# Softmax attention beside a SwiGLU feed-forward on one core: odd score pairs in two single PSUM banks, and a plan of 108 blocks in place of 115

## The chip, the cores and the metric

The kernel runs on one core of one Trainium2 chip. The metric is device time in microseconds (us), the median of several executions. The engines that matter here are TensorE (PE in the profile; PEld is its loading of weights), ScalarE (ACT), VectorE (DVE), GpSimd (POOL) and SyncE (SP), whose queue issues most DMA transfers. PSUM, where matmuls leave their results, has eight banks of 512 float32 values per partition.

## What is computed

The input `x` has 2048 rows (tokens) of 512 features. With `xn` the layer-normed `x`, the output is `x + s * g`:

```python
qkv = xn @ wqkv                           # 32 heads, 16 features each
p = softmax(q @ k.T * 16 ** -0.5)         # per head, 2048 x 2048
s = (p @ v, heads side by side) @ wo
g = silu((silu(xn @ w_gate) * (xn @ w_up)) @ w_down)   # 512 -> 1792 -> 512
```

All tensors are float32. The feed-forward and the projections use matmuls on a high and a low part of each operand (three products for one), so that a reduced-precision pass gives nearly full precision.

## The kernel before

**Stages.** A prologue (the first score matmul is at 157.6 us) normalises `x`, transposes it and projects q, k and v to DRAM. A long middle stretch runs attention and the feed-forward together on TensorE. A short tail does the last quarter of the output projection.

**Attention.** The heads are taken four at a time (8 groups), the queries 512 at a time (4 blocks of queries); one such combination is a *unit*, and there are 32. A unit goes over 16 *key tiles* of 128 keys. For each key tile there are two *pairs* (j = 0, 1; "even" and "odd" below) of two heads each. The two scores of a pair are two matmuls that run at the same time, on the upper and the lower half of the array's rows (line 899), one PSUM bank each. ScalarE turns scores into exponentials in SBUF (`pr`). Then `values` (line 423) multiplies the exponentials of a key tile with v: four heads at once in the four column quarters of the array, in float32, accumulated in the bank `acc`.

**PSUM in the middle stretch.** `bankx` and `banky` belong to the feed-forward, `acc` to `values`. `score[0]` and `score[1]` have two banks each: even pairs go to `score[0]`, odd pairs to `score[1]`. `spare` is one bank. An ordinary pair is read by one ACTIVATE over both banks, 128x1024 (line 902). A pair that is `apart` (the last of its block, or one in `shared`) puts its first half in `room[:, 0]` and its second half in `spare`, and each half is read for itself, 128x512.

**Kept-back halves.** For a pair in `shared`, one half gets no exponential at once: VectorE copies the scores to SBUF (line 907) so that the bank comes free, and ScalarE does that exponential from SBUF at the end of the block (line 920, after the loop over pairs). This is the second half of the pair, or the first half if the pair is the block's last.

**Fills.** The feed-forward is a generator; `fill(n)` draws n *fills* from it, each a pair of 64-row matmuls into `bankx` and `banky` (line 237). An up unit (one slice of 128 of the 1792 hidden features) has 24 fills and ends in a tanh on ScalarE (line 264) and four VectorE operations (lines 265, 266, 230, 231). A down unit (128 tokens through `w_down`) has 21. At the start of an up unit VectorE splits the next gate and up weights (`split_gu`, lines 198 and 199), and after eight fills it splits a slice of `w_down` (`split_wd`, lines 208 and 209). A down unit that finishes its 128 tokens leaves `store_gate` in `after` (a tanh on ScalarE, a multiply on VectorE, a store on GpSimd's queue); the last four leave `next_out` as well, which splits parts for the output projection on VectorE. `catch_up` runs what is in `after` before pair 2 of the next block.

**Blocks and the plan.** The stretch is cut into *blocks* of 2 to 6 key tiles of one unit. In a block, TensorE does: scores of pairs 0 and 1; `values` of the block before; then pairs 2 to the last, and after pair n the number of fills `parts[n]`. So ScalarE works off pairs 0 and 1 and the kept-back halves of the block before while TensorE is in `values`. Below, a *turn* is the passage through `values`: into it after pair 1, and out of it to pair 2. I write (k, n) for a block of k key tiles and n fills. `plan()` chooses the blocks by dynamic programming: 327 per block, plus `short(k, n)` for a block with few fills for its tiles, or a small price where the table `SHARED` has an entry for (k, n), which says which pairs are shared and where the fills go. Without an entry the fills are spread evenly. The planner's rule, followed through, gives 115 blocks: 28 of (6,24), 24 of (5,24), 22 of (5,21), 14 of (2,6), 10 of (4,15), 10 of (3,12), 4 of (2,12), 2 of (2,9) and the first, (4,20).

**Other order.** Each engine runs its instructions in the order in which the code issues them. `turn_acc` and `finish` (VectorE transposes and scaling of a finished unit) come in the first block of the next unit, behind pair 2k-3 and behind the last pair. Keys, queries and values are fetched by SP ahead of the unit that needs them.

Of the kernel before, what the change touches and what calls it, by code (L numbers as in the profile page):

```python
# [9 lines left out]
F32 = mybir.dt.float32  # L10
# [3 lines left out]
AF = mybir.ActivationFunctionType  # L14
# [5 lines left out]
P = 128  # L20
# [6 lines left out]
TB = S // NB  # L27
# [20 lines left out]
SHARED = {  # L48
# [3 lines left out]
}  # L52
# [5 lines left out]
def plan():  # L58
# [17 lines left out]
    short = lambda k, n: 15 * len(SHARED[k, n][0]) if (k, n) in SHARED else 250 * max(0, 6 * (k - 1) - n)  # L76
    ways = {at: {} for at in range(start, stop + 1)}
    ways[start][ends[0]] = 0, None
    for at in range(start, stop):
        room = KT - at % KT  # L80
        for done, (cost, _) in ways[at].items():
            rem = next((n for n in ends if n > done), done) - done
            for k in SIZES:
                for n in [rem] + list(range(3, rem - 2)):
# [5 lines left out]
                    c = cost + 327 + short(k, n) + (650 if n == rem and k == 2 else 0) + abs(n - 4.1 * k) / 2  # L90
                    if to[1] not in ways[to[0]] or ways[to[0]][to[1]][0] > c:
                        ways[to[0]][to[1]] = c, (at, done, k, n)
# [3 lines left out]
    cost = lambda r: ways[stop - r][ends[-1]][0] + sum(short(k, n) for k, n in zip(pairs[r], rest))  # L96
    r = min((r for r in pairs if ends[-1] in ways[stop - r]), key=cost)
    middle, step = [], ways[stop - r][ends[-1]][1]
    while step:
        middle.insert(0, step[2:])  # L100
        step = ways[step[0]][step[1]][1]
# [12 lines left out]
def tile_block(ctx: ExitStack, tc: tile.TileContext, x, wqkv, wo, w_gate, w_up, w_down, out):  # L114
# [131 lines left out]
    def ffn(b):  # L246
        for grp, part in enumerate(GROUPS):
# [31 lines left out]
            for t in range(NT):  # L279
                n = 0  # L280
                for f in range(nf):
                    for a, w in ((0, 0), (0, 1), (1, 0)):
# [9 lines left out]
                        elif n == 3 * nf:  # L292
# [3 lines left out]
                            after.append(partial(store_gate, y, b * TB + t * P))  # L296
                            if b == NB - 1:
                                after.append(partial(next_out, t))
                        yield 3 * nf - n
# [552 lines left out]
    score = [spool.tile([P, 2, 512], F32, name=f"score{i}") for i in range(2)]  # L852
# [11 lines left out]
    for u in range(units):  # L864
# [3 lines left out]
        for now in range(begin[u], begin[u + 1]):  # L868
# [10 lines left out]
            for n in range(2 * size):  # L879
# [16 lines left out]
                apart = last_pair or n in shared  # L896
                for h in range(2):
                    r = slice(h * HALF, h * HALF + NROW)
                    mm(spare if apart and h else room[:, h], k[r, j, kc * P:(kc + 1) * P], q[r, j], start=True, stop=True)  # L899
                pr = ppool.tile([P, 2, TB], F32, tag="pr", name="pr")  # L900
                if not apart:
                    exps.append(act(pr, room, AF.Exp, scale=0.25))  # L902

                for h in range(2) if apart else ():
                    src = spare if h else room[:, 0]
# [111 lines left out]
```

## Time and profile before

| what | value |
|---|---|
| median of 3 runs | 1396.45 us (1396.27 to 1398.05) |
| span of the profiled execution, first to last instruction | 1394.9 us |
| granted TensorE clock, mean | 0.999 |
| DVE busy | 689.8 us (49%) |
| ACT busy | 1108.9 us (79%) |
| POOL busy | 89.5 us (6%) |

The profile gives no other time for that execution than its span; the median is 1.55 us above the span, for what lies around the first and the last instruction and for the difference between executions. Times in the trace are counted from the start of the span. PE's busy time counts each matmul up to a modelled end, so PE looks busy nearly all the time; where it loses time is to be read from the starts of its instructions.

### The profile page before, as it was taken

To read this page: it belongs to the slowest core of one execution; us is meant where nothing else is said; L and a number is where in the kernel's file an instruction comes from. 1 tells how busy PE (TensorE), PEld (TensorE's weight loads), DVE (VectorE), ACT (ScalarE), POOL (GpSimd) and SP (SyncE) were. 2 spreads that over 40 slices of the span, in tenths; PEclk is the share of its full clock that TensorE was granted. 3 is DMA by queue.
4 is the path that set the end of the run, shared out by engine and by line. 5 is a ranking of instruction groups with operands and counts; after the bars stand their busy time and mean duration, and the time that the engine had idled before them with its cause. 6 is when DMAs were issued, how large, how long until landed. Compare 5 with 4: busy or idle time off the path is not lost.

```text
span 1394.9 us, 27065 instructions
## 1 busy us (share of the span) xinstructions
PE 1388.4 (100%) x11197; PEld 835.5 (60%) x11197; DVE 689.8 (49%) x1126; ACT 1108.9 (79%) x1516; POOL 89.5 (6%) x102
## 2 busy tenths in 40 slices
PE   9999999999999999999999999999999999999998
PEld 7788655556555655565565555656556556555554
DVE  5643454254534563455356434644455434554645
ACT  6733587888888888888888888888888888888774
POOL 4200100000000000000000000000000000000254
PEclk9999999999999999999999999999999999999999
DMA  7778541134453511245533302257234302233642
GB/s 237 263 250 268 144 115 43 35 69 111 107 129 81 134 43 36 51 103 111 128 83 102 98 13 51 67 134 156 65 81 113 79 15 59 61 83 105 196 151 107
DMA packets 128687, 149.16 MB, mean 107 GB/s; under 512 B 12593, under 2 KB 80689, under 8 KB 127790
## 3 DMA queue, kind: packets, MB, share of 16 engines
q1 hardware_dynamic: 123246, 126.72, 36.1%
q0 software_dynamic: 4880, 20.12, 3.9%
q8 instruction: 89, 1.46, 0.5%
q10 hardware_dynamic: 432, 0.52, 0.1%
q14 instruction: 40, 0.33, 0.1%
HBM read 107.46 MB, written 40.11 MB: 106 GB/s over the span
## 4 chain that ended last, share of the span: by engine, by line
PE 87%; ACT 1%; DVE 1%; issue 0%; DVEq 0%; ACTq 0%
PE acc L423 32%; PE bankx L237 29%; PE score L899 18%; PE banky L237 7%; PE spare L899 1%; ACT pr L902 0%; PE spare L955 0%; PE banky L955 0%; PE score L955 0%; DVE hh L231 0%; DVE pr L907 0%; DVE gul L199 0%; ACT pr L910 0%; DVE hh L230 0%; DVE y L962 0%
## 5 line engine op out<-in xcount | busy, mean ns | idle before, releaser
L902 ACT ACTIVATE pr<-score 128x1024 f32<-128x1024 f32 x743 | 722.5, 1029 | 95.8 <-PE score L899 86.2
L423 PE MATMUL acc<-pr,vst 128*17 128x512 f32 x4096 | 461.8, 593 | 0.0
L899 PE MATMUL score<-qst,kst 50*128 50x512 f32 x1767 | 406.9, 407 | 0.4 <-ACT pr L902 0.4
L237 PE MATMUL bankx<-fx,guh 64*128 64x512 f32 x896 | 303.3, 392 | 0.2 <-PEq L810 0.2
L237 PE MATMUL banky<-fx,guh 64*128 64x512 f32 x896 | 303.2, 392 | 0.0
L899 PEld LDWEIGHTS score<-qst,kst 50*128 50x128 f32 x1767 | 193.3, 184 | 161.9 <-ACT pr L902 66.0
L423 PEld LDWEIGHTS acc<-pr,vst 128*17 128x17 f32 x4096 | 110.3, 97 | 280.4 <-issue 272.3
L907 DVE COPY pr<-spare 128x512 f32<-128x512 f32 x166 | 114.3, 689 | 249.5 <-PE spare L899 188.5
L910 ACT ACTIVATE pr<-score 128x512 f32<-128x512 f32 x221 | 131.7, 596 | 100.2 <-PE spare L899 72.2
L237 PE MATMUL bankx<-wd,hh 64*128 64x512 f32 x672 | 197.1, 392 | 0.0
L237 PE MATMUL banky<-wd,hh 64*128 64x512 f32 x672 | 197.1, 392 | 0.0
L237 PEld LDWEIGHTS bankx<-fx,guh 64*128 64x128 f32 x896 | 167.0, 187 | 26.7 <-issue 0.9
L237 PE MATMUL banky<-fx,gul 64*128 64x512 f32 x448 | 175.3, 391 | 0.0
L237 PE MATMUL bankx<-fx,gul 64*128 64x512 f32 x448 | 175.3, 391 | 0.0
L237 PEld LDWEIGHTS banky<-fx,guh 64*128 64x128 f32 x896 | 167.1, 187 | 3.2
L265 DVE SCALAR_TENSOR_TENSOR ga<-th,bankx 128x512 f32<-128x512 f32 x56 | 38.5, 687 | 201.4 <-ACT th L264 201.4
L237 PEld LDWEIGHTS bankx<-wd,hh 64*128 64x128 f32 x672 | 125.2, 186 | 18.6
L237 PEld LDWEIGHTS banky<-wd,hh 64*128 64x128 f32 x672 | 125.2, 186 | 5.9
L920 ACT ACTIVATE pr<-pr 128x512 f32<-128x512 f32 x226 | 124.2, 633 | 0.0
L899 PE MATMUL spare<-qst,kst 50*128 50x512 f32 x281 | 118.0, 420 | 0.2 <-DVE pr L907 0.2
L237 PEld LDWEIGHTS bankx<-fx,gul 64*128 64x128 f32 x448 | 83.0, 185 | 13.5
L237 PEld LDWEIGHTS banky<-fx,gul 64*128 64x128 f32 x448 | 83.0, 185 | 1.6
(171 smaller groups left out, 1400.8 us busy)
## 6 DMA issues: line engine op xcount, KB each, us to landing
gur<-in_B_w_gate_dram SPq DMA_DIRECT2D x56, 256.0 KB
gur<-in_B_w_up_dram SPq DMA_DIRECT2D x56, 256.0 KB
wdr<-in_B_w_down_dram SPq DMA_DIRECT2D x56, 256.0 KB
kst<-k_d SPq DMA_DIRECT2D x192, 64.0 KB
qst<-q_d SPq DMA_DIRECT2D x192, 64.0 KB
fx<-xt_d SPq DMA_DIRECT2D x24, 512.0 KB
q_d<-parts SPq DMA_DIRECT2D x16, 512.0 KB
k_d<-parts SPq DMA_DIRECT2D x16, 512.0 KB
```

Of the source, the lines that this page charges most:

```text
L237: mm(bank, lhs[h], rhs[h], start=start, stop=stop)
L265: dve.scalar_tensor_tensor(ga, th, 1.0, bankx, op0=ALU.add, op1=ALU.mult)
L423: mm(acc[h * 32:h * 32 + DH + 1], v[:, kt % CT, h * (DH + 1):(h + 1) * (DH + 1)], probs[2 * i + h // 2][:, h % 2], start=kt == 0, stop=kt ...
L899: mm(spare if apart and h else room[:, h], k[r, j, kc * P:(kc + 1) * P], q[r, j], start=True, stop=True)
L902: exps.append(act(pr, room, AF.Exp, scale=0.25))
L907: dve.tensor_copy(pr[:, h], src)
L910: exps.append(act(pr[:, h], src, AF.Exp, scale=0.25))
L920: exps.append(act(part, part, AF.Exp, scale=0.25))
```

## The change

Odd pairs get two separate one-bank tiles instead of one two-bank tile, and are always read by two 128x512 ACTIVATEs, one for each half. `spare` is now used only by the last pair of a block and by even pairs in `shared`; an odd pair in `shared` is copied out of its own second bank. `SHARED` gets new entries and new patterns: (6,24) now shares pairs 4, 6, 7, 8, 9 (before 2, 5, 7, 9, 11), (5,21) shares 2, 5, 6, 7, and (3,12), (4,15), (4,18), (5,24), (6,21) have entries. The planner's prices change, and it remembers the size of the block before, so that two short six-tile blocks in a row can be priced. The new rule, followed through, gives 108 blocks: 41 of (6,24), 16 of (5,21), 11 of (4,24), 10 of (3,12), 9 of (6,21), 7 of (2,6), 4 of (4,21), 4 of (2,12), 3 of (4,15), 2 of (2,9) and the first, (4,20). Six tiles beside a down unit, (6,21), did not occur before; there a down unit was mostly cut into (2,6) and (4,15). The last down units put `next_out` ahead of `store_gate`.

```diff
--- before.py
+++ after.py
@@ -46,9 +46,13 @@
 
 
 SHARED = {
-    (4, 15): ((2, 7), (1, 3, 3, 3, 2, 3)),
-    (5, 21): ((2, 7, 9), (1, 3, 3, 3, 3, 2, 2, 4)),
-    (6, 24): ((2, 5, 7, 9, 11), (1, 3, 3, 2, 3, 2, 2, 3, 1, 4)),
+    (3, 12): ((5,), (3, 2, 3, 4)),
+    (4, 15): ((2, 5, 7), (1, 3, 3, 3, 1, 4)),
+    (4, 18): ((7,), (3, 3, 3, 3, 2, 4)),
+    (5, 21): ((2, 5, 6, 7), (0, 4, 3, 3, 1, 3, 2, 5)),
+    (5, 24): ((6, 9), (2, 4, 3, 3, 3, 2, 3, 4)),
+    (6, 21): ((2, 4, 5, 7, 8, 9), (1, 3, 2, 1, 3, 2, 2, 1, 3, 3)),
+    (6, 24): ((4, 6, 7, 8, 9), (3, 2, 3, 3, 2, 2, 2, 1, 3, 3)),
 }
 EPS = 1e-5
 QSLOT = (0, 1, 0)
@@ -73,12 +77,12 @@
     units = H // 4 * NB
     start, stop = sum(k for k, _ in first), (units - 2) * KT
     pace = (ends[-1] - ends[0]) / (stop - start)
-    short = lambda k, n: 15 * len(SHARED[k, n][0]) if (k, n) in SHARED else 250 * max(0, 6 * (k - 1) - n)
+    short = lambda k, n: 60 if (k, n) in SHARED else 250 * max(0, 6 * (k - 1) - n)
     ways = {at: {} for at in range(start, stop + 1)}
-    ways[start][ends[0]] = 0, None
+    ways[start][ends[0], 4] = 0, None
     for at in range(start, stop):
         room = KT - at % KT
-        for done, (cost, _) in ways[at].items():
+        for (done, last), (cost, _) in ways[at].items():
             rem = next((n for n in ends if n > done), done) - done
             for k in SIZES:
                 for n in [rem] + list(range(3, rem - 2)):
@@ -87,18 +91,19 @@
                         continue
                     if abs(to[1] - ends[0] - (to[0] - start) * pace) > 45:
                         continue
-                    c = cost + 327 + short(k, n) + (650 if n == rem and k == 2 else 0) + abs(n - 4.1 * k) / 2
-                    if to[1] not in ways[to[0]] or ways[to[0]][to[1]][0] > c:
-                        ways[to[0]][to[1]] = c, (at, done, k, n)
+                    c = cost + 327 + short(k, n) + (120 if k == 6 and n < 24 else 0) + (700 if k == last == 6 and n < 24 else 0) + (650 if n == rem and k == 2 else 0) + abs(n - 4.1 * k) / 2
+                    if (to[1], k) not in ways[to[0]] or ways[to[0]][to[1], k][0] > c:
+                        ways[to[0]][to[1], k] = c, ((at, (done, last)), (k, n))
 
     rest = [3 * (DT - 1)] * EARLY
     pairs = {4: (2, 2), 5: (3, 2), 6: (3, 3)}
-    cost = lambda r: ways[stop - r][ends[-1]][0] + sum(short(k, n) for k, n in zip(pairs[r], rest))
-    r = min((r for r in pairs if ends[-1] in ways[stop - r]), key=cost)
-    middle, step = [], ways[stop - r][ends[-1]][1]
+    best = lambda r: min((w[0], key) for key, w in ways[stop - r].items() if key[0] == ends[-1])
+    cost = lambda r: best(r)[0] + sum(short(k, n) for k, n in zip(pairs[r], rest))
+    r = min((r for r in pairs if any(done == ends[-1] for done, _ in ways[stop - r])), key=cost)
+    middle, step = [], ways[stop - r][best(r)[1]][1]
     while step:
-        middle.insert(0, step[2:])
-        step = ways[step[0]][step[1]][1]
+        middle.insert(0, step[1])
+        step = ways[step[0][0]][step[0][1]][1]
     rest += [3 * DT] * (NT * (NB - 1))
     parts = []
     for k, n in first + middle + list(zip(pairs[r] + 2 * LAST, rest)):
@@ -293,9 +298,9 @@
                             y = two.tile([P, D], F32, tag="ga", name="y")
                             dve.tensor_add(y, bankx, facc[:, t])
                             dve.tensor_add(y, banky, y)
-                            after.append(partial(store_gate, y, b * TB + t * P))
                             if b == NB - 1:
                                 after.append(partial(next_out, t))
+                            after.append(partial(store_gate, y, b * TB + t * P))
                         yield 3 * nf - n
 
 
@@ -849,7 +854,8 @@
     hh = att.tile([P, FG, 2, TB], F32R, name="hh")
     wd = att.tile([P, FG, 2, D], F32R, name="wd")
     spare = spool.tile([P, 512], F32, name="spare")
-    score = [spool.tile([P, 2, 512], F32, name=f"score{i}") for i in range(2)]
+    both_banks = spool.tile([P, 2, 512], F32, name="score0")
+    score = [[both_banks[:, h] for h in range(2)], [spool.tile([P, 512], F32, name=f"single{h}") for h in range(2)]]
     ring(2, RING, att)
     queries(1, att)
     gate = [w.rearrange("p f j t -> p (f j) t")[:, 12 + i].bitcast(F32) for w in (hh, wd) for i in range(2)]
@@ -894,22 +900,22 @@
 
                 room, last_pair = score[j], n == 2 * size - 1
                 apart = last_pair or n in shared
+                banked = room[0], spare if last_pair or apart and not j else room[1]
                 for h in range(2):
                     r = slice(h * HALF, h * HALF + NROW)
-                    mm(spare if apart and h else room[:, h], k[r, j, kc * P:(kc + 1) * P], q[r, j], start=True, stop=True)
+                    mm(banked[h], k[r, j, kc * P:(kc + 1) * P], q[r, j], start=True, stop=True)
                 pr = ppool.tile([P, 2, TB], F32, tag="pr", name="pr")
-                if not apart:
-                    exps.append(act(pr, room, AF.Exp, scale=0.25))
-
-                for h in range(2) if apart else ():
-                    src = spare if h else room[:, 0]
+                if not apart and not j:
+                    exps.append(act(pr, both_banks, AF.Exp, scale=0.25))
+
+                for h in range(2) if apart or j else ():
                     if n in shared and h != last_pair:
-                        dve.tensor_copy(pr[:, h], src)
+                        dve.tensor_copy(pr[:, h], banked[h])
                         kept_back.append(pr[:, h])
                     else:
-                        exps.append(act(pr[:, h], src, AF.Exp, scale=0.25))
+                        exps.append(act(pr[:, h], banked[h], AF.Exp, scale=0.25))
                 if n == 1 and now:
-                    tc.add_manual_dep(exps[-1].ins, exps[-3].ins.name, settled, reason="order of the slots' writes")
+                    tc.add_manual_dep(exps[-2].ins, exps[-4].ins.name, settled, reason="order of the slots' writes")
                 probs.append(pr)
                 if ended is not None and n == max(2, 2 * size - 3):
                     o1 = turn_acc(0, TB)
@@ -941,7 +947,7 @@
     assert not queue and not after and given == total
     hi = two.tile([P, 2, D], F32R, tag="guh", name="rh")[:, 0]
     lo = one.tile([P, D], F32R, tag="th", name="rl")
-    outs = (score[0][:, 0], score[1][:, 0], spare, banky)
+    outs = (score[0][0], score[1][0], spare, banky)
     half = TB // 2
     cols = [slice(n * half, (n + 1) * half) for n in range(2)]
     room, *y = [ppool.tile([P, 2, TB], F32, tag="pr", name="y") for _ in range(3)]
```

## The prediction, made before the result was known

> **What bounds the kernel now.** I read the chain's shares on the page first, then the chain in order of time and the starts of TensorE's instructions, then what ScalarE and VectorE do beside them.
>
> ```profile
> PE 87%; ACT 1%; DVE 1%; issue 0%; DVEq 0%; ACTq 0%
> ```
>
> The chain stays on PE for 87% of the span, on ACT and DVE for 1% each, and the change leaves the number of matmuls as it is. What can be won is time that PE loses between matmuls, so that is measured first. One slot (a score pair or a fill) and one turn, from PE's timeline in a (5,24) block:
>
> ```profile
> 595.11 0.39 PE L237 MATMUL bankx<-fx,guh 64*128 64x512 f32 x1
> ...
> 602.38 0.64 PE L899 MATMUL score<-qst,kst 50*128 50x512 f32 x4
> 602.95 0.62 PE L423 MATMUL acc<-pr,vst 128*17 128x512 f32 x4
> ```
>
> From 595.11 to 602.38 stand 24 fills and 7 score pairs: 7.27 / 31 = 0.2345 us a slot. The two pairs ahead of `values` take 0.57 (602.38 to 602.95) where two slots are 0.47: so a turn costs something by itself. How much in all, the next rows tell. Whole blocks come from the chain, which gives the start of each run of `values`:
>
> ```profile
> 219.17 4.42 PE acc L423 x40
> 231.80 0.61 PE score L899 x4
> 232.41 5.28 PE acc L423 x48
> ...
> 360.84 4.42 PE acc L423 x40
> 373.93 5.28 PE acc L423 x48
> 386.64 4.42 PE acc L423 x40
> 393.12 0.48 PE score L899 x4
> 393.60 1.84 PE acc L423 x16
> 400.55 0.58 PE score L899 x4
> 401.14 3.56 PE acc L423 x32
> 412.13 4.42 PE acc L423 x40
> 424.03 4.42 PE acc L423 x40
> 436.65 4.42 PE acc L423 x40
> 448.73 0.48 PE score L899 x4
> 449.21 4.42 PE acc L423 x40
> ```
>
> x16 and x48 are two and six key tiles, so a tile takes (5.28 - 1.84) / 4 = 0.86 us. From one start to the next lie the tiles of the block before and 2k + n slots of this one. What is left over is the turn and its waits:
> - (5,24), 436.65 to 449.21: 12.56 - 34 x 0.2345 - 4.30 = **0.29**, which I take as the bare turn.
> - (5,21), 412.13 to 424.03: 11.90 - 7.27 - 4.30 = 0.33. (2,6), 386.64 to 393.60: 6.96 - 2.35 - 4.30 = 0.31.
> - (4,15), 393.60 to 401.14: 7.54 - 5.39 - 1.72 = 0.43, so 0.14 of waits.
> - (6,24) inside a unit, 360.84 to 373.93: 13.09 - 8.44 - 4.30 = 0.35, so 0.06. (6,24) that closes a unit, 219.17 to 232.41: 13.24 - 12.74 = 0.50, so 0.21.
>
> The whole stretch, from the first `values` to the last:
>
> ```profile
> L423 PE MATMUL acc<-pr,vst x4096: 592/592/606, 165.9 to 1382.1; 128*17 128x512 f32 x196
> ```
>
> It lasts 1382.1 + 0.43 (half a tile, the last pass) - 165.9 = 1216.6 us. In it are 512 tiles (440.3) and, by the plan behind the first block, 1016 pairs and 2130 fills (3146 x 0.2345 = 737.7). That leaves 38.6 us for 115 turns: 33.4 of bare turns and **5.2 us of waits**, net of blocks that come out a little under 0.29. More than turns and waits the change cannot win.
>
> **The change, part by part.** *Seven turns fewer.* 108 blocks carry the same tiles, pairs and fills: 7 x 0.29 = **-2.0 us**.
>
> *Waits that go.* Of the 28 old (6,24), 15 close a unit, 12 do not, and one is block 1: 15 x 0.21 + 12 x 0.06 = 3.9; ten (4,15) give 1.4. Block 1 waits for VectorE, which at that time still has work of the prologue's last fills:
>
> ```profile
> 172.19 1.23 DVE L199 TENSOR_TENSOR gul<-gur,guh 128x1024 fp32r<-128x1024 f32 x1
> 173.34 0.68 DVE L907 COPY pr<-spare 128x512 f32<-128x512 f32 x1
> ```
>
> The copy of pair 5 stands behind the weight split, and `spare` behind the copy; the same queue holds up the next copy. I put block 1 at 0.9. Together 6.2, where the whole stretch shows 5.2 net. I book half of the difference on these blocks, whose single rows may overstate, and half on blocks under 0.29, which stay: **-5.7 us**.
>
> *Splitting every odd pair.* How many full and kept-back ACTIVATEs there are, and ScalarE's pace when one follows another at once:
>
> ```profile
> L902 ACT ACTIVATE pr<-score 128x1024 f32<-128x1024 f32 x743 | 722.5, 1029 | 95.8 <-PE score L899 86.2
> ...
> L920 ACT ACTIVATE pr<-pr 128x512 f32<-128x512 f32 x226 | 124.2, 633 | 0.0
> ```
> ```profile
> 616.15 2.72 ACT L920 ACTIVATE pr<-pr 128x512 f32<-128x512 f32 x5
> 618.75 1.94 ACT L902 ACTIVATE pr<-score 128x1024 f32<-128x1024 f32 x2
> ```
> ```profile
> 601.88 0.60 ACT L910 ACTIVATE pr<-score 128x512 f32<-128x512 f32 x1
> ...
> 602.37 0.59 ACT L910 ACTIVATE pr<-spare 128x512 f32<-128x512 f32 x1
> 602.38 0.64 PE L899 MATMUL score<-qst,kst 50*128 50x512 f32 x4
> 602.52 0.18 PEld L899 LDWEIGHTS score<-qst,kst 50*128 50x128 f32 x2 [0.19 <-ACT pr L910]
> 602.85 0.61 ACT L264 ACTIVATE th<-bankx 128x512 f32<-128x512 f32 x1
> ```
>
> A full one takes 1.94 - 1.03 = 0.91 of ScalarE's time (the mean of 1.029 overlaps the next), a half 0.49 and 0.48 (601.88, 602.37, 602.85), one from SBUF (2.72 - 0.63) / 4 = 0.52. By the new plan 743 full ones become 327, 336 halves (by the old plan) become 1052, 226 kept-back ones 342: -416 x 0.91 + 716 x 0.48 + 116 x 0.52 = +25 us on ScalarE. What hides it: ACT is busy for 1108.9 of 1394.9 us.
>
> ```profile
> 165.80:1380.90 1215.10, 1214.91 (x10374) 700.28 (x10376) 599.02 (x922) 1019.89 (x1367) 52.77 (x61) 1.00 0.36 89
> ```
>
> That row (the stretch; columns PE, PEld, DVE, ACT, POOL, clock, DMA) leaves ScalarE 195 us idle and VectorE 616; 116 more copies of about 0.69 add 80 us to VectorE. So in sum both have room, and only the order inside a block can cost.
>
> The Trainium skill, Perfetto Trace Analysis, section "Optimizing Scalar/DVE Operations", has two rules here: larger grouped operations help if the engine is saturated, and breaking up instructions may help if it isn't but holds up another engine. The second speaks for the change, the first against it; the idle 195 us fit the second. The same skill's page ScalarE: Activation LUTs, section "What ACT_TABLE_LOAD costs", gives 186 ns + 0.833 ns an element and 93 ns of overlap, so about 0.95 for a full one and 0.52 for a half, as estimates; the rows show less, and by the page ScalarE's addition would be about 38 us instead of 25.
>
> *The new (6,24), by hand.* PE starts pair 2 at time 0; the next slot comes at about 0.33 (0.10 late out of `values`, as the two pairs above were going in). A score is ready for ScalarE 0.44 after its start: the pair read at 601.88 started four slots before 602.38. A bank takes its next score 0.14 after the ACTIVATE's end: 601.88 + 0.60 = 602.48, weights at 602.52, and the last matmul of the x4 row starts at 602.38 + 0.64 - 0.40 = 602.62. An ACTIVATE ends 0.60 (half) or 1.03 (full) after its start. Pair 3's second half ends at 2.55, pair 5 could start at 2.66: 0.03 late. Pair 5's second half ends at 4.22, pair 7 could start at 4.33: 0.03 late. Pair 10 and the next block's pair 1 come out 0.01 late each. The old late point is gone: pair 10's ACTIVATE has three fills, pair 11 and three fills behind it, as pair 8 has in the (5,24) that showed the bare turn. So about 0.07 a block, whether or not it closes a unit; 41 x 0.07 = 2.9. *(6,21)* has gaps of two fills or fewer behind six of its pairs and six kept-back halves; the nearest row is (4,15), also short of fills, with 0.14, and I take 0.12: 9 x 0.12 = 1.1. (4,24) and (4,21) have four fills a pair, (5,21) and the last (3,12) are like rows with next to nothing. Block 1: the first copy is now pair 4's, behind the split, 0.3. New waits **+4.3 us**; at the least none, at the most what the rivals below say.
>
> *The order of `next_out` and `store_gate`* touches four turns of the last 100 us, and their blocks stand at the bare turn in today's sum; the splits it moves (some 2 us of VectorE) come earlier, the tanh and the store of the gate by as much later, under five tiles of other work. Zero; without that cover 4 x 0.3 either way.
>
> Sum: -2.0 - 5.7 + 4.3 = -3.4. On the profiled execution's span that gives 1394.9 - 3.4 = 1391.5; the 1.55 us from span to median stay, so **1393.1 us**.
>
> **The rivals.**
> - *All waits vanish.* Halves free their bank sooner, and the bare turn is all that is left: 1396.45 - 2.0 - 5.7 = 1388.8. For it: the late steps in my block are hundredths. Against: they are chained, and each old six-tile block has some.
> - *Six-tile blocks keep today's wait.* Then 17 new closing ones at 0.21, 24 at 0.06, nine (6,21) at 0.14 and block 1 at 0.3 give 6.6: 1396.45 - 2.0 - 5.7 + 6.6 = 1395.4, no change. For it: nothing but the hand-worked cadence says that the closing blocks lose their 0.15.
> - *VectorE is late: slower.* Pairs 6, 7, 8, 9 each need a copy within a slot or two, and the split of `w_down` stands among them:
>
> ```profile
> 610.40 0.68 DVE L907 COPY pr<-spare 128x512 f32<-128x512 f32 x1
> 611.00 0.42 DVE L208 CAST wd<-wdr 128x512 fp32r<-128x512 f32 x1
> 611.45 0.69 DVE L209 TENSOR_TENSOR wd<-wdr,wd 128x512 fp32r<-128x512 f32 x1
> 612.06 0.68 DVE L907 COPY pr<-spare 128x512 f32<-128x512 f32 x1
> ```
>
>   The split holds VectorE for 1.06 (611.00 to 612.06). In the new block pair 4's copy and the split take 0.60 + 1.06 = 1.66 from 0.47 behind pair 4; pair 6 is ready for its copy at 8 x 0.2345 + 0.47 = 2.35, so there is 0.2 to spare, and 0.1 more before pair 8 needs `spare`. If the split slips more than that (its weights land late), copies 6 and 7 are late by up to 0.8. In one of four of the 41: 10 x 0.8 = +8, so 1401; it decides from about four such blocks on, which eat up the gain. Against it: above, the split follows its copy at once, so its data were there.
> - *ScalarE paces it.* The 25 us come on the path: 1396.45 - 2.0 + 25 = 1419. Against: the idle 195 us. The Trainium skill's rule on grouping, named above, would end here if ScalarE were full.
>
> **How the numbers follow.** Forecast 0.50 (own range 1391.0 to 1394.9), all waits vanish 0.13, no change 0.20, VectorE late 0.14, ScalarE paces 0.03. The bound for "same" is 0.2%, 2.8 us, about what a measurement of this kernel can tell from none: 1393.7 to 1399.2. The forecast lies on both sides of it, 0.43 below and 0.07 above. Faster 0.13 + 0.43 = 0.56; same 0.20 + 0.07 = 0.27; slower 0.17. Low: 1389.2, just above the floor of 1388.8. High: into the case of late copies, seven of them instead of ten, 1393.1 + 5.6 = 1398.7. Outside lie about 0.02 below, and above 0.14 x 0.7 + 0.03.
>
> **What would show it.** 108 runs of `values` and 327 full ACTIVATEs; (6,24) from start to start at most 0.10 above the bare turn, also where it closes a unit; ScalarE's last halves and kept-back ones done before `values` needs them. The sum is wrong if the bare turn isn't 0.29 in blocks of six; the steps are wrong if PE waits behind copies of pairs 6 to 9.

## The result, and the profile after

The changed kernel takes **1393.68 us** (median of 10 runs, 1393.37 to 1394.31); before, on the same chip, 1396.55 (1396.27 to 1398.05). The ratio is 0.9979, 95% interval 0.9971 to 0.9986: 2.9 us or 0.2% faster. Forecast were 1393.1 us, or 3.35 less; the time came 0.6 us above that. The experiments show that several of the forecast's terms missed by more, and that their errors nearly cancelled.

The page of the changed kernel: span, busy time of the engines, the chain's shares by engine, and the groups of ScalarE's exponentials (line 909 full, 916 halves, 926 kept back; the row of 916 is for the `single` banks, two more are for `score` and `spare`).

```profile
span 1391.9 us, 27666 instructions
...
PE 1383.6 (99%) x11197; PEld 863.9 (62%) x11197; DVE 772.5 (56%) x1242; ACT 1155.7 (83%) x1932; POOL 89.4 (6%) x102
...
PE 86%; DVE 2%; ACT 1%; issue 0%; DVEq 0%
...
L916 ACT ACTIVATE pr<-single 128x512 f32<-128x512 f32 x759 | 427.7, 605 | 19.9 <-PE spare L906 3.1
L909 ACT ACTIVATE pr<-score 128x1024 f32<-128x1024 f32 x327 | 337.1, 1031 | 90.3 <-PE score L906 86.7
...
L926 ACT ACTIVATE pr<-pr 128x512 f32<-128x512 f32 x342 | 187.2, 641 | 1.3 <-DVE pr L913 1.3
```

The chain still stays on PE. There are 327 full exponentials as counted ahead; VectorE has 772.5 - 689.8 = 83 us more (80 were forecast).

Two views carry the time: the row of all matmuls of `values` (now line 428), and the starts of their runs in the chain.

```profile
L428 PE MATMUL acc<-pr,vst x4096: 592/592/607, 165.5 to 1379.1; 128*17 128x512 f32 x196
```
```profile
206.27 3.56 PE acc L428 x32
...
218.49 5.27 PE acc L428 x48
...
232.44 5.28 PE acc L428 x48
...
245.13 4.42 PE acc L428 x40
...
256.96 4.42 PE acc L428 x40
...
269.39 5.28 PE acc L428 x48
```

The stretch lasts 1379.1 + 0.43 - 165.5 = 1214.0 us; less the same 440.3 for tiles and 737.7 for slots, 36.0 are left for 108 turns (before: 38.6 for 115). Both counts of slots are two pairs, 0.47 us, too high, because behind the last block no next block's pairs 0 and 1 stand ahead of `values`. So the row "the rest" in the table below is 0.47 too low in every column, and so are the sums; no difference between kernels changes. By the prediction's measure, 0.2345 us a slot and 0.86 a tile:

- (6,24) inside a unit, 206.27 to 218.49: 12.22 - 8.44 - 3.44 = 0.34. (6,24) that closes a unit, 218.49 to 232.44: 13.95 - 8.44 - 5.16 = 0.35, where the old one, 219.17 to 232.41, had 0.50.
- (5,21), 245.13 to 256.96: 11.83 - 7.27 - 4.30 = 0.26. (6,21), 256.96 to 269.39: 12.43 - 7.74 - 4.30 = 0.39.

The same subtraction for every block, less 0.29 for the bare turn, gives the waits in us by kind of block (a negative number: blocks shorter than the bare turn). Besides before and after it shows three kernels of the experiments below.

| blocks | before | new banks alone | + new patterns, old blocks | after | after + two edits |
|---|---|---|---|---|---|
| (6,24) inside a unit | 0.59 (12) | 0.87 | 0.49 | 1.00 (23) | 0.97 |
| (6,24) closing a unit | 2.70 (15) | 2.59 | 0.77 | 0.98 (17) | 0.99 |
| block 1, (6,24) | 0.92 | 0.98 | 1.92 | 1.45 | 0.59 |
| (6,21) | none | none | none | 0.95 (9) | 0.93 |
| (5,24) and (5,21) | -0.07 (46) | 3.71 | -1.25 | -0.60 (16) | -0.63 |
| (4,15) | 1.17 (10) | 1.15 | -0.01 | 0.02 (3) | 0.00 |
| (3,12) | 0.30 (10) | 0.54 | 1.45 | 1.46 (10) | 0.27 |
| the rest | -0.04 | -0.11 | -0.06 | -0.37 | -0.39 |
| sum of waits | 5.57 | 9.73 | 3.31 | 4.89 | 2.73 |
| bare turns between first and last | 33.06 (114) | 33.06 | 33.06 | 31.03 (107) | 31.03 |
| turns and waits | **38.6** | **42.8** | **36.4** | **35.9** | **33.8** |

From before to after the stretch wins 2.7 us. The span wins 3.0; the other 0.3 lie ahead of the stretch, whose start (165.9, now 165.5) falls anywhere from 165.3 to 166.1 in the kernels traced here, in no order, so these 0.3 look like chance.

Two rows got worse, and their loss sits in three blocks. In block 1, the second of the stretch, VectorE's rows and the one of PE that waits:

```profile
172.45 0.68 DVE L913 COPY pr<-spare 128x512 f32<-128x512 f32 x1
173.64 0.43 DVE L213 CAST wd<-wdr 128x512 fp32r<-128x512 f32 x1 [0.50 <-DMA wdr<-in_B_w_down_dram]
174.10 0.69 DVE L214 TENSOR_TENSOR wd<-wdr,wd 128x512 fp32r<-128x512 f32 x1
174.71 0.68 DVE L913 COPY pr<-spare 128x512 f32<-128x512 f32 x1
```
```profile
175.49 0.47 PE L906 MATMUL spare<-qst,kst 50*128 50x512 f32 x1 [0.64 <-issue]
```

VectorE is free, but its next instruction is the split of `w_down`, whose weights land at 173.6. The copy out of `spare` stands behind it, and PE's next score for `spare` starts 1.03 after the matmul ahead of it.

In block 102, one of the (3,12) near the end:

```profile
1341.53 0.71 DVE L453 STREAM_TRANSPOSE o<-on 128x512 f32<-128x512 f32 x1
1342.27 0.43 DVE L334 CAST hh<-o 128x512 fp32r<-128x512 f32 x1
1342.74 0.69 DVE L335 TENSOR_TENSOR hh<-o,hh 128x512 fp32r<-128x512 f32 x1
1343.35 0.68 DVE L913 COPY pr<-single 128x512 f32<-128x512 f32 x1
```
```profile
1344.08 0.50 PE L906 MATMUL single<-qst,kst 50*128 50x512 f32 x2 [0.70 <-DVE pr L913]
```

VectorE works without a pause on the finished unit and the split for the output projection; the copy of the shared pair 5 comes last, and PE, whose last start was 1342.98, waits 1.10. Block 97 loses 0.3 in the same way.

### The profile page after: what moved, and what is told of

Same layout as the page of the kernel before. It is cut to its first block, busy times and chain, and to the rows that moved or that the text cites. A ratio compares the mean times of both kernels' runs of the same rounds, so it can differ in the third digit from the quotient of the medians.

```text
span 1391.9 us, 27666 instructions
## 1 busy us (share of the span) xinstructions
PE 1383.6 (99%) x11197; PEld 863.9 (62%) x11197; DVE 772.5 (56%) x1242; ACT 1155.7 (83%) x1932; POOL 89.4 (6%) x102
## 4 chain that ended last, share of the span: by engine, by line
PE 86%; DVE 2%; ACT 1%; issue 0%; DVEq 0%
PE acc L428 32%; PE bankx L242 29%; PE score L906 9%; PE single L906 8%; PE banky L242 6%; PE spare L906 1%; ACT pr L916 0%; ACT pr L909 0%; PE spare L961 0%; PE banky L961 0%; DVE pr L913 0%; DVE gul L204 0%; DVE wd L335 0%; DVE wd L334 0%; DVE on L446 0%
## 5 line engine op out<-in xcount | busy, mean ns | idle before, releaser
L916 ACT ACTIVATE pr<-single 128x512 f32<-128x512 f32 x759 | 427.7, 605 | 19.9 <-PE spare L906 3.1
L909 ACT ACTIVATE pr<-score 128x1024 f32<-128x1024 f32 x327 | 337.1, 1031 | 90.3 <-PE score L906 86.7
L913 DVE COPY pr<-spare 128x512 f32<-128x512 f32 x185 | 127.9, 691 | 169.0 <-PE spare L906 156.8
L906 PE MATMUL score<-qst,kst 50*128 50x512 f32 x839 | 218.9, 419 | 0.0
L906 PE MATMUL single<-qst,kst 50*128 50x512 f32 x916 | 212.9, 399 | 0.8 <-DVE pr L913 0.7
L926 ACT ACTIVATE pr<-pr 128x512 f32<-128x512 f32 x342 | 187.2, 641 | 1.3 <-DVE pr L913 1.3
L906 PEld LDWEIGHTS score<-qst,kst 50*128 50x128 f32 x839 | 98.2, 184 | 118.4 <-ACT pr L916 77.1
L913 DVE COPY pr<-single 128x512 f32<-128x512 f32 x157 | 108.4, 691 | 64.8 <-PE single L906 36.9
L916 ACT ACTIVATE pr<-score 128x512 f32<-128x512 f32 x185 | 111.4, 602 | 34.9 <-PE spare L906 27.5
L906 PEld LDWEIGHTS single<-qst,kst 50*128 50x128 f32 x916 | 114.0, 184 | 26.5 <-ACT pr L916 8.3
```

The source lines that it names most:

```text
L906: mm(banked[h], k[r, j, kc * P:(kc + 1) * P], q[r, j], start=True, stop=True)
L909: exps.append(act(pr, both_banks, AF.Exp, scale=0.25))
L913: dve.tensor_copy(pr[:, h], banked[h])
L916: exps.append(act(pr[:, h], banked[h], AF.Exp, scale=0.25))
L926: exps.append(act(part, part, AF.Exp, scale=0.25))
```

## The experiments

My theory after the result: the gain comes from the banks and patterns together and from the turns, and single blocks in which VectorE is late give part of it back. Rivals: the plan is the gain; the patterns are; or the splitting costs time that the plan wins back. Each kernel is compared with before on its own chip, where before took 1396.67 to 1397.17 us; so the ratios are what to compare.

**The new banks alone.** The changed code with the old table and plan.

```diff
...
-    (5, 24): ((6, 9), (2, 4, 3, 3, 3, 2, 3, 4)),
-    (6, 21): ((2, 4, 5, 7, 8, 9), (1, 3, 2, 1, 3, 2, 2, 1, 3, 3)),
-    (6, 24): ((4, 6, 7, 8, 9), (3, 2, 3, 3, 2, 2, 2, 1, 3, 3)),
+    (4, 15): ((2, 7), (1, 3, 3, 3, 2, 3)),
+    (5, 21): ((2, 7, 9), (1, 3, 3, 3, 3, 2, 2, 4)),
+    (6, 24): ((2, 5, 7, 9, 11), (1, 3, 3, 2, 3, 2, 2, 3, 1, 4)),
...
```

> The changed kernel with the plan and the table of before: odd pairs in two single banks, but 115 blocks and the old shared pairs. My theory (the gain is seven bare turns of 0.29 us, 2.0 us, and the new cadence of fills at the end of the six-tile blocks): both are gone, so about the time of before, 1396.0 us, between 1395.3 and 1397.0; six-tile blocks that close a unit still 0.1 or more longer than the others. Rival (the separate banks free halves sooner and win by themselves): 1394.5 us or less with 115 blocks. Rival (the added ACTIVATEs cost): 1398 us or more.

1401.43 us, ratio 1.0037 (1.0023 to 1.0051): 4.8 us *slower* than before. The rival held. Of the 4.2 us that the stretch loses, 3.8 are in the (5,24) and (5,21). ScalarE in a (5,24) with three fills behind every pair:

```profile
430.08 1.03 ACT L904 ACTIVATE pr<-score 128x1024 f32<-128x1024 f32 x1 [1.47 <-PE score L901]
431.01 1.09 ACT L911 ACTIVATE pr<-single 128x512 f32<-128x512 f32 x2
431.98 1.03 ACT L904 ACTIVATE pr<-score 128x1024 f32<-128x1024 f32 x1
432.89 1.10 ACT L911 ACTIVATE pr<-single 128x512 f32<-128x512 f32 x2
433.86 1.05 ACT L904 ACTIVATE pr<-score 128x1024 f32<-128x1024 f32 x1
```

No row behind the first has idle time ahead of it. An even and an odd pair take 431.98 - 430.08 = 1.90 us, the next two 1.88; TensorE comes with two pairs and six fills every 8 x 0.2345 = 1.876. ScalarE has nothing to spare there, though it is busy for 80% of the span. TensorE then waits for it: in the (5,24), whose turns are 0.08 longer each, where pair 1 of the next block needs the bank of the last pair, and in the (5,21), 0.08 longer too, at pair 8:

```profile
422.59 0.19 PEld L901 LDWEIGHTS score<-qst,kst 50*128 50x128 f32 x2 [0.19 <-ACT pr L904]
...
437.35 0.19 PEld L901 LDWEIGHTS single<-qst,kst 50*128 50x128 f32 x2 [0.26 <-ACT pr L911]
```

**New banks and patterns, old blocks.** The planner and its table `SHARED` are the old ones, so the 115 blocks of before; the new table, as `PATTERNS`, says which pairs are shared and where the fills go.

```diff
+PATTERNS = {
...
-        shared, behind = SHARED.get((k, n), ((), even))
+        shared, behind = PATTERNS.get((k, n), ((), even))
```

> The changed kernel with the 115 blocks of before in their old order, but with the new table's patterns in them: (6,24), (5,21), (4,15), (3,12) as in the changed kernel, and (5,24) with halves of pairs 6 and 9 kept back. My theory (split odd pairs put ScalarE at the pace of three fills a pair, and the new patterns take it off that pace; the rest of the gain is the number of turns): what the old plan with old patterns lost, 4.8 us against before, is won back by the patterns; the turns are those of before, so 1395 to 1397 us. Rival (the plan's choice of blocks matters, five-tile blocks are bad with split pairs whatever the pattern): 1399 us or more. Rival (patterns are the whole gain): 1393.7 us.

1394.40 us, ratio 0.9979 (0.9970 to 0.9988): the changed kernel's ratio, without its plan. The expectation missed and the rival on the patterns held. In the table, the patterns take the five-tile blocks from 3.7 us of waits to -1.3 (a (5,24) now shares two pairs, so ScalarE has two halves fewer among its pairs), the closing (6,24) from 2.6 to 0.8 and the (4,15) from 1.2 to none.

**The new plan and patterns, old banks.** The kernel before with the new table and planner.

```diff
-    (6, 24): ((2, 5, 7, 9, 11), (1, 3, 3, 2, 3, 2, 2, 3, 1, 4)),
...
+    (6, 21): ((2, 4, 5, 7, 8, 9), (1, 3, 2, 1, 3, 2, 2, 1, 3, 3)),
+    (6, 24): ((4, 6, 7, 8, 9), (3, 2, 3, 3, 2, 2, 2, 1, 3, 3)),
```

> The kernel of before (odd pairs in one two-bank tile, kept-back halves all through the one bank spare) with the new plan and table: 108 blocks. My theory (the new patterns need the separate banks, since in (6,24) four pairs in a row, 6 to 9, keep a half back, and spare is free again only 0.47 + 0.69 + 0.11 = 1.27 us after its score while the pairs come every 0.70): about 0.57 us of waiting at three pairs of each (6,24) and like amounts in (5,21) and (6,21): 60 to 100 us slower than before, 1455 to 1500 us. Rival (the plan alone makes the gain and the banks are not needed): 1394 us.

1511.91 us in a single run, where before took 1397.17: 115 more (60 to 100 were expected). So "the plan alone" fell. Where TensorE's weight loads and matmuls wait:

```profile
PEld spare L904 <- DVE pr L912: 126.1, 183, 1.9
...
PE spare L904 <- DVE pr L912: 47.8, 117, 1.5
```

Pairs 6 to 9 all want `spare`; each waits for the copy of the one before. Patterns with neighbouring shared pairs need the two banks.

**Eleven turns more.** Each (4,24) becomes two (2,12), which have the bare turn.

```diff
+    parts = [p for k, s, f in parts for p in ([(2, (), [0, 0, 6, 6])] * 2 if (k, sum(f)) == (4, 24) else [(k, s, f)])]
```

> The changed kernel with each of the eleven (4,24) cut into two (2,12): 119 blocks, same tiles, pairs and fills. My theory (a bare turn costs 0.29 us of TensorE whatever surrounds it): 11 x 0.29 = 3.2 us more than the changed kernel, 1396.9 us, between 1396.4 and 1397.5. Rival (the number of turns costs nothing, only waits for other engines do): no difference, 1393.7 us. Rival (short blocks leave ScalarE without work in values and pay it back): 1399 us or more.

1401.06 us, ratio 1.0028 (1.0017 to 1.0038), some 6.8 us above the changed kernel: twice the expectation. The trace divides it. The 22 (2,12) come to 6.36 us where the eleven (4,24) came to 2.96: 3.40, or 0.31 a turn, as expected. The other 3.5 sit in the eleven (6,24) that now come behind a two-tile block: their turn is 0.6 to 0.7 instead of 0.3 to 0.4.

```profile
213.92 0.42 DVE L214 CAST wd<-wdr 128x512 fp32r<-128x512 f32 x1
214.37 0.69 DVE L215 TENSOR_TENSOR wd<-wdr,wd 128x512 fp32r<-128x512 f32 x1
214.98 0.68 DVE L914 COPY pr<-spare 128x512 f32<-128x512 f32 x1
```
```profile
215.72 0.18 PEld L907 LDWEIGHTS spare<-qst,kst 50*128 50x128 f32 x1 [0.29 <-DVE pr L914]
```

With `values` 1.84 us long instead of 3.56, VectorE's work for the up unit runs into the block's pairs; the copy of pair 6 stands behind the split, and the second half of pair 8, which needs `spare` again, waits for the copy of pair 6. The recorded rival on short blocks has the number (1399 or more), but its cause, ScalarE, is not the one that these rows show. It is the prediction's rival of late copies, at 0.32 a block.

**No (6,21).** The plan then falls back on 115 blocks.

```diff
-    (6, 21): ((2, 4, 5, 7, 8, 9), (1, 3, 2, 1, 3, 2, 2, 1, 3, 3)),
```

> The changed kernel without the table entry for six tiles beside a down unit, (6,21); the planner then makes 115 blocks, with 41 of (6,24) as in the changed kernel and (2,6), (4,15), (5,21) in place of the nine (6,21). My theory (a turn costs 0.29 us, and a (6,21) pays 0.11 of waits): 7 x 0.29 - 9 x 0.11 = 1.0 us more than the changed kernel, 1394.7 us, between 1394.2 and 1395.2. Rival (the seven turns are the whole gain): 2.9 us more, 1396.5 us. Rival (the plan's number of blocks does not matter, the patterns of (6,24) do): no difference, 1393.7 us.

1396.36 us, ratio 0.9996 (0.9987 to 1.0005), about 2.4 above the changed kernel; 1.0 was expected, and the rival that makes the seven turns the whole gain had 2.9. The trace divides it otherwise. The stretch holds 2.5 more. Of these, 1.0 are one (5,21) that closes a unit and 0.3 block 1; 1.2 remain for the seven turns more and the waits that go with (6,21), near the 1.0 expected. In that (5,21) the scores of the next unit's pair 0:

```profile
688.41 0.47 PE L905 MATMUL score<-qst,kst 50*128 50x512 f32 x1
689.13 0.47 PE L905 MATMUL score<-qst,kst 50*128 50x512 f32 x1 [0.24 <-DMA qst<-sh_d]
```

The second half waits for queries that land late: the chain has their transfer from 687.35 to 688.99. A plan also decides when a unit's loads start.

**Even pairs split too**, in four single banks.

```diff
-    both_banks = spool.tile([P, 2, 512], F32, name="score0")
-    score = [[both_banks[:, h] for h in range(2)], [spool.tile([P, 512], F32, name=f"single{h}") for h in range(2)]]
+    score = [[spool.tile([P, 512], F32, name=f"single{j}{h}") for h in range(2)] for j in range(2)]
...
-                for h in range(2) if apart or j else ():
+                for h in range(2):
```

> The changed kernel with the even pairs split too: four single banks, and two 128x512 ACTIVATEs for each pair, some 320 ACTIVATEs more, 15 to 20 us more work for ScalarE. My theory as it stands after the run with the old plan (ScalarE has 160 us to spare in sum, but sets the pace in stretches with three fills a pair; only pairs 2 to 5 of the (6,24) are such): 0.03 to 0.08 us in each of 41 (6,24), 1 to 3 us more than the changed kernel, 1394.7 to 1396.7 us. Rival (idle time hides it all): 1393.7 us. Rival (ScalarE is full and larger operations are better throughout): 1408 us or more.

1396.92 us, ratio 0.9997 (0.9988 to 1.0006): 2.5 above the changed kernel, inside the expectation of 1 to 3. The gain is gone. The page's group of halves:

```profile
L912 ACT ACTIVATE pr<-single 128x512 f32<-128x512 f32 x1598 | 840.9, 614 | 131.2 <-PE single L905 87.3
```
The loss is spread: 0.06 in each (6,21) and (4,21), 0.04 in each (2,6), 0.03 in each (6,24). TensorE's waits for ScalarE's exponentials don't show it as a sum: 87.2 us for the single banks here, 92.3 for `score` and the single banks in the changed kernel. So that ScalarE's pace is the cause in these blocks is argued from the run with the old pattern, not read off.

**Block 1 with the old pattern.**

```diff
+    parts[1] = 6, (2, 5, 7, 9, 11), [0, 0, 1, 3, 3, 2, 3, 2, 2, 3, 1, 4]
```

> The changed kernel, but block 1 alone, the first (6,24), has its old pattern (pairs 2, 5, 7, 9, 11 shared). My theory (the new pattern puts the w_down split, whose weights land late only here, ahead of the copies of pairs 6 and 7): block 1 falls from 13.62 us back towards the 13.1 of before, 0.4 to 0.6 us less in all, about 1393.2 us. Rival (block 1 is slow because of what the prologue leaves behind, whatever the pattern): 13.6 us in block 1 and 1393.7 us in all.

1393.65 us, ratio 0.9978 (0.9969 to 0.9987), nothing won; block 1 has 1.76 of turn and wait where it had 1.74. The old pattern by itself doesn't bring block 1's time back. VectorE there:

```profile
174.36 0.43 DVE L214 CAST wd<-wdr 128x512 fp32r<-128x512 f32 x1 [0.39 <-DMA wdr<-in_B_w_down_dram]
```

The split waits for its weights under either pattern, here until 3.42 us after their issue at 170.94. In the run with the new banks alone, the same old pattern had its split at 174.25, 2.95 after the issue and without a wait, and block 1 lost 0.98. So the landing counts. In the eight traces with the new pattern or plan and the split after eight fills, the wait ends 2.9 to 3.4 us after the issue; why it differs from one to the next is open, and so is the pattern's own share.

**The last (3,12) without a shared pair.**

```diff
+    for i in range(94, len(parts)):
+        k, _, p = parts[i]
+        parts[i] = (k, (), [0, 0] + [sum(p) // (2 * k - 2)] * (2 * k - 2)) if k == 3 else parts[i]
```

> The changed kernel, but the last eight (3,12) blocks, beside the output projection, keep no half back and have three fills behind each pair, as before the change. My theory (a late copy on VectorE, behind splits and scaling of the output projection, holds the last score pair up in two of these blocks, for 1.0 and 0.33 us): 1.0 to 1.4 us less than the changed kernel, so about 1392.5 us, and no run of values more than 0.1 above its neighbours of the same shape there. Rival (those two blocks wait for something else, such as a transfer, that the kept-back half only makes visible): no difference, 1393.7 us.

1393.22 us, ratio 0.9974 (0.9964 to 0.9984). The (3,12) go from 1.46 us of waits to 0.49, as the theory has it; the median wins some 0.7 against the changed kernel where 1.0 to 1.4 were expected, and in this profile block 1 took 0.3 more.

**The old order: `store_gate` ahead of `next_out`.**

```diff
+                            after.append(partial(store_gate, y, b * TB + t * P))
                             if b == NB - 1:
                                 after.append(partial(next_out, t))
-                            after.append(partial(store_gate, y, b * TB + t * P))
```

> The changed kernel with the old order of the last four down units' tasks: store_gate ahead of next_out. My theory (four turns, with VectorE's splits hidden either way): no difference from the changed kernel beyond 0.5 us, 1393.2 to 1394.2 us. Rival (the tanh of the gate holds VectorE for up to 3 us ahead of the splits and of a kept-back copy, as it did in the run without (6,21), block 46): 1 us or more slower, 1394.7 us or above.

1395.73 us, ratio 0.9990 (0.9981 to 0.9999). "No difference" fell. One block, number 91, a (6,21), carries it: 2.23 where it had 0.41. VectorE with the old order, and the PE row that waits:

```profile
1257.89 0.69 DVE L300 TENSOR_TENSOR y<-banky,y 128x512 f32<-128x512 f32 x1
1261.74 0.69 DVE L247 SCALAR_TENSOR_TENSOR y<-th,y 128x512 f32<-128x512 f32 x1 [3.15 <-ACT th L246]
1262.34 0.42 DVE L334 CAST part<-pair 128x512 fp32r<-128x512 f32 x1
...
1263.86 0.69 DVE L315 TENSOR_TENSOR fx<-wor,fx 128x512 fp32r<-128x512 f32 x1
1264.47 0.68 DVE L913 COPY pr<-spare 128x512 f32<-128x512 f32 x1
```
```profile
1265.21 0.50 PE L906 MATMUL spare<-qst,kst 50*128 50x512 f32 x1 [1.45 <-DVE pr L913]
```

And VectorE in the changed kernel at the same place:

```profile
1257.99 0.69 DVE L300 TENSOR_TENSOR y<-banky,y 128x512 f32<-128x512 f32 x1
1258.60 0.42 DVE L334 CAST part<-pair 128x512 fp32r<-128x512 f32 x1
...
1261.85 0.69 DVE L247 SCALAR_TENSOR_TENSOR y<-th,y 128x512 f32<-128x512 f32 x1 [1.04 <-ACT th L246]
1262.56 0.69 DVE L913 COPY pr<-spare 128x512 f32<-128x512 f32 x1
```

The multiply of `store_gate` waits for its tanh, which ScalarE does after the kept-back halves. With the old order VectorE idles for 3.15 us and then does the four splits ahead of the copy of pair 2; with the new order the splits fill the idle time. The old kernel paid nothing there, because in its plan a (2,6), which shares no pair, follows this down unit. Behind the first of the four down units both plans have a (5,21) that shares pair 2; there one split stands ahead of the copy, and no time is lost in either order.

**Both stalls removed.** The split of `w_down` in block 1 (and the load of the next slice behind it) after 16 fills instead of 8, and blocks 97 and 102 without a shared pair.

```diff
+    for i in (97, 102):
+        parts[i] = 3, (), [0, 0, 3, 3, 3, 3]
-                        if i and n == (DC if i > 1 else 3 * DC):
+                        if i and n == (DC if i > 2 else 2 * DC if i == 2 else 3 * DC):
```

> The changed kernel with its two single stalls taken out: blocks 97 and 102, beside the output projection, keep no half back, and in block 1 the w_down split comes after 16 fills instead of 8, so that VectorE does not stand behind late weights ahead of the copies. My theory (both are VectorE being late for a copy that a score bank waits for): 1.2 to 1.3 us from the two blocks and 0.7 to 1.3 us from block 1, 1391.4 us, between 1391.0 and 1391.9; block 1 at 12.9 us or less. Rival (block 1 waits for something else): 1392.4 us.

1391.98 us, ratio 0.9963 (0.9949 to 0.9977): 5.2 us below before; no kernel here is faster beyond the noise. Block 1's wait falls from 1.45 to 0.59, the (3,12) from 1.46 to 0.27. VectorE in block 1:

```profile
172.84 0.68 DVE L915 COPY pr<-spare 128x512 f32<-128x512 f32 x1
174.12 0.69 DVE L915 COPY pr<-spare 128x512 f32<-128x512 f32 x1 [0.59 <-PE spare L908]
...
176.13 0.42 DVE L215 CAST wd<-wdr 128x512 fp32r<-128x512 f32 x1
```

Now VectorE waits for a score, not for weights, and the split comes when its weights are there.

**Do 108 blocks beat 115, once those stalls are gone?** The kernel with the old blocks gets the same two edits (there the two (3,12) are blocks 104 and 109); the kernel with both edits runs once more beside it.

```diff
+    for i in (104, 109):
+        parts[i] = 3, (), [0, 0, 3, 3, 3, 3]
```

> The 115 blocks of the plan before, with the new banks and patterns, and with the single stalls taken out as in the kernel that beat both (the two (3,12) behind next_out shared no more, the first w_down split eight fills later). Theory: a turn saved is worth 0.30 us, but the 108 blocks pay it back, because a six-tile block loses 0.07 more and a (6,21) 0.13 more than a five-tile one: 7 x 0.33 = 2.3 saved against 13 x 0.07 + 9 x 0.13 = 2.1 spent. Then the time is that of the 108 blocks with the same two edits, within 0.7 us, on the same chip: ratio to before 0.9955 to 0.9970. Rival: the seven turns do count once the single stalls are gone; then this kernel is 2.0 us slower than the 108 blocks.

> The 108 blocks with both edits once more, on the same chip as the 115 blocks with both edits, to compare the two plans. All theories: ratio to before 0.9963 as measured, 0.9955 to 0.9970. The first theory expects the 115 blocks within 0.7 us of it, the rival 2.0 us above it.

115 blocks: 1391.97 us, ratio 0.9964 (0.9950 to 0.9978). 108 blocks: 1391.63, ratio 0.9961 (0.9947 to 0.9975). They are 0.3 us apart, and so are their stretches (34.05 and 33.75 for turns and waits). The theory held, and the rival, 2.0 us, fell.

## Why the prediction was right, and where it was not

The stretch went from 38.6 to 35.9 us of turns and waits where 38.6 - 3.4 = 35.2 were forecast. Term by term:

- **Seven turns fewer, -2.0: right in size, not as a gain.** A turn is worth 0.31, shown by adding eleven. The seven come from down units: of 32, the old plan does 22 whole, as (5,21), and cuts ten in two; the new one cuts three. But the plan pays for the seven turns with 13 more (6,24) and nine (6,21) in place of 24 (5,24) and six (5,21), above all: with the stalls gone, waits are 2.73 against 0.99 with the old blocks (34.05 - 114 x 0.29), so 1.7 of 2.0 is paid back. The prediction's sum has these waits as a term of their own, but sets them against the waits of the old patterns; it never asks what the old blocks would wait with the new patterns.
- **Waits that go, -5.7: right.** The old (6,24), block 1 and the (4,15) held 0.59 + 2.70 + 0.92 + 1.17 = 5.4. The single rows did overstate, as the prediction suspected; but half of the gap between its 6.2 and 5.2 was the two pairs counted too many.
- **New waits of six-tile blocks: right.** (6,24) 0.05 each (0.07 forecast), also where they close a unit, but for block 2, which still has 0.21; (6,21) 0.11 (0.12). By the mean starts of the pairs in the other (6,24), 0.03 of it arises from pair 4 to pair 6, near the step that was worked out for pair 5; the step at pair 7 did not come. The rival that six-tile blocks keep today's wait fell; "all waits vanish" fell too.
- **Splitting every odd pair at nothing: wrong as it was argued.** The 195 us that ScalarE idles in sum do not cover it: with the old patterns the split costs 4.8 us, because at three fills a pair the two halves bring ScalarE to 1.88 to 1.90 us for every 1.876 of TensorE. The sum was too small as well: ScalarE's busy time rose by 46.8 us, not 25; a half that stands alone takes 0.60 of it, not the 0.48 of one behind another. What hides it is the patterns, which keep halves back until `values`. The two rules of the Trainium skill, Perfetto Trace Analysis, section "Optimizing Scalar/DVE Operations", both show here: breaking up helped where it freed a bank (0.9979 with patterns), and grouping was right where the pace was full (1.0037 without; 0.9997 with even pairs split too). "Saturated" must be read for the stretch of a block, not for the span.
- **Block 1 at 0.3: wrong in direction.** It was 0.92 and became 1.45. The step that failed put only the gate and up split ahead of pair 4's copy; of the split of `w_down` the prediction says, from a block in the middle, that "its data were there". In block 1 they land late, and the copy of pair 6 stands behind: moving the split by eight fills brings 0.59, where the old pattern alone brought nothing.
- **(3,12) at next to nothing: wrong by 1.2**, in two blocks. The step that failed took the old (3,12) as like rows, but those share no pair. In the new ones the copy of pair 5 stands behind the finished unit's work (block 102) and behind splits that took long beside GpSimd (block 97).
- **The order of `next_out` and `store_gate` at zero: right in the sum, wrong for the edit.** Neither before nor after has a stall there. But in the changed kernel the old order would cost 1.8. The cover that the prediction named, five tiles of other work, is TensorE's; on VectorE the copy of pair 2 of the new (6,21) is queued behind both. The prediction priced the edit against the old kernel, where a (2,6) without a copy stands in that place.
- **The rival of late copies (1401)** had the right mechanism. It needed some ten blocks at 0.8; it came in three, for 0.5, 0.3 and 1.0 more than they should have had.

So the sum missed the stretch by only 0.7 because errors of both signs nearly cancelled, and the time by less because of the 0.3 ahead of the stretch: that it came so near is in part luck. Too dear were the waits of the new (6,24) (2.9 forecast, 1.98 found) and (6,21), by 1.1 together, and the shapes costed at nothing, (5,21), (4,24) and the two-tile ones above all, came 0.9 below the like rows of before. Too cheap were block 1 and the (3,12), by 1.2 each, and the waits that go were 0.3 fewer: 1.2 + 1.2 + 0.3 - 1.1 - 0.9 = 0.7. How much of block 1's remaining 0.59 could go was not tried.

## What to carry to other kernels

Whether an engine has room is decided over the few microseconds in which its work must keep up with the bottleneck; write its work per period beside the bottleneck's period, and count idle time only there. When an instruction is added to an in-order queue, look at every place where it occurs for what may stand ahead of it and wait for something else (a transfer, another engine): three such places in 108 blocks kept this change at 2.9 us, where 5 were to be had. And when a planner trades a fixed price for a larger piece, subtract the larger piece's own price before booking the gain: seven turns fewer were worth 0.3 us here, not 2.

## What the runs showed of the hardware

Some of VectorE's operations between SBUF tiles became up to 3.6 times as long while GpSimd was adding. VectorE in block 97, and GpSimd at the same time:

```profile
1305.34 0.42 DVE L334 CAST wd<-wd 128x512 fp32r<-128x512 f32 x1
1305.79 1.69 DVE L335 TENSOR_TENSOR wd<-wd 128x512 fp32r<-128x512 f32 x1
1307.40 1.52 DVE L334 CAST wd<-wd 128x512 fp32r<-128x512 f32 x1
1308.95 0.69 DVE L335 TENSOR_TENSOR wd<-wd 128x512 fp32r<-128x512 f32 x1
```
```profile
1305.64 1.28 POOL L386 TENSOR_TENSOR y<-y,fx 128x512 f32<-128x512 f32 x1 [14.56 <-ACT pr L916]
1307.01 1.63 POOL L387 TENSOR_TENSOR pair<-y,pair 128x512 f32<-128x512 f32 x1
```

The same subtract takes 0.69 alone and 1.69 beside GpSimd's addition, the same cast 0.42 (mostly ahead of it) and 1.52; the two long ones end 0.56 and 0.28 after GpSimd's instructions do. In the whole trace, five of the seven such subtractions of lines 334 and 335 that overlap GpSimd take 1.65 to 1.69 and two of the seven casts 1.52; the others keep their time, as do all 342 of VectorE's copies out of PSUM (line 913, 0.68 to 0.69). The Trainium skill, SBUF — State Buffer, section "Who interferes with whom", says that VectorE shares one pair of ports with GpSimd as an exclusive lock, for instructions with two SBUF inputs or in a two-port mode; the long rows agree. They hold VectorE 2.1 us longer ahead of block 97's copy, which starts at 1309.56, when its score is half a microsecond old. That it would have come in time without GpSimd is worked out from these rows, not tried.
